# Where the attention's softmax rows are divided by their sums: on VectorE before the transposition, instead of on x^T after it

## The chip, the core and the metric

The kernel runs on one core of a Trainium2 chip. A core has five engines with a queue of instructions each: TensorE (PE, with its weight loads shown as PEld), VectorE (DVE), ScalarE (ACT), GpSimd (POOL) and SyncE (SP), which here issues nearly all DMAs. The engines run side by side and wait for each other only through semaphores. The metric is the device time of one execution in microseconds (us); lower is better.

## The reference

Three stages follow each other: causal attention with a decay for 2 batches of 8 heads, then a mixture of eight experts with weights from eight rounds of normalization, then a second mixture that sends each token to two experts. The change touches the first stage only:

```
scores = scale * q @ k^T + (cum[:, None] - cum[None, :])     # 576 x 576 for a head, future masked
attn = exp(scores - rowmax)
attn = attn / (attn.sum(-1) + 1e-09)
x = attn @ v                                                  # 576 x 64 for a head
```

The result of the sixteen heads, as rows of 512, is the input x of the first mixture.

## The kernel before

A head's 576 rows are five tiles (four of 128 rows and one of 64). Tile t keeps the columns up to its own diagonal, so it is 128, 256, 384, 512 or 576 wide, and it lies in the buffer P of its head (two buffers, for even and odd heads). For each tile PE multiplies q by k (`score_mm`, L253, in two parts for precision), VectorE adds the decay and takes the row minimum of the negated scores (`score_max`, L281, named CUSTOM_DVE in the trace and ISA in the program order), and ScalarE takes the exponential and sums it along the row (`score_exp`, L286). PE then transposes the tiles (`turn_mm`, L343) into PSUM tiles t, of which there are two: the first transposition of a head takes tiles 0 and 1 together, the next three take tiles 2, 3 and 4. ScalarE rounds what was transposed (`turn_hi`, L355), VectorE takes the remainder (`turn_lo`, L359), and only then is t free. PE multiplies by the parts of v (`value_mm`, L372), and VectorE collects x^T of two heads, a pair, in xf (`value_add`, L383).

The x^T of a pair is not yet divided. The sums of a head's rows lie along partitions, but x^T needs their reciprocals along the free axis. So `recip` (L323, L324) makes the reciprocals in a tile rs (two buffers), SP sends them to DRAM as single numbers of 4 bytes (L325, L326), `bcast` reads them back spread over 64 partitions (L332), and `x_mul` (L388) multiplies, on GpSimd for seven pairs and on VectorE for the last. Then `x_parts` (L397, L398) splits x^T into two rounded parts. GpSimd also splits q (`split_q`, L248, L249) and v (`split_v`, L235, L236).

The order on every engine is written out by hand: `at(time, fn)` puts each step at a place in fifths of a head, five to a head, and the steps are issued sorted by place. Engines work their queues strictly in that order. From head 10 on, PE also works on the first expert's first 384 tokens (`fill_mm`, L131 to L133, with names o<-xh,w1h), between the steps of the heads. When the last pair's x^T is split, PE goes on with the logits of the first gate (L567, L568) and the experts, which take the rest of the time.

Of the kernel before, what the change touches and what calls it, by code (L numbers as in the profile page):

```python
# [10 lines left out]
F32 = mybir.dt.float32  # L11
# [4 lines left out]
OP = mybir.AluOpType  # L16
# [4 lines left out]
# places of the attention's instructions, in fifths of a head's time  # L21
# [8 lines left out]
D_RECIP = 1.9  # L30
D_VAL = [[3.6, 4.8, 5.81, 5.82], [5.8, 6.2, 7.3, 7.66]]
D_X = [5.35, 9.05, 9.65]
D_SPLITV = 3.95
D_CONV = 1.25
# and of the first gate's, in us
T_GATE = [0.4, 1.85, 3.3, 3.55, 3.8, 1.8]
# and of the routing's after a tile's, in us
T_ROUTE = [[1.45, 1.8, 3.0, 5.75, 11.65, 0.4, 4.2], [2.0, 3.7, 4.0, 5.9, 6.85, 2.15, 5.55], [1.05, 1.6, 2.65, 6.2, 7.4, 0.4, 3.9], [1.0, 1.15, 2.3, 5.4, 7.15, 3.5, 0.6]]
# of the weights' conversions there, and of the first list's transposes
# [7 lines left out]
def attn_moe_moe2_kernel(ctx: ExitStack, tc: tile.TileContext, q, k, v, f, wg1, w1, w2,  # L47
                         wg2, wn2, noise, w21, w22, out, dbg=None):
    nc = tc.nc
# [5 lines left out]
    # slots of the second mixture's lists: of the first expert's tokens, early and late, and the others' in  # L55
    # the order of their length
# [25 lines left out]
    rscr = nc.dram_tensor("r_scratch", (B * H, S), F32, kind="Internal").ap()  # L82
# [52 lines left out]
    # what the gates need  # L135
# [19 lines left out]
    # ---------------------------------------------------------------- attention  # L155
    def attention():
        with ExitStack() as c2:
# [7 lines left out]
            # buffers with parts that stay zero  # L165
# [8 lines left out]
            def load_head(p, nm, hs, tail=True, views=(0, 1)):  # L174
                """rows of some heads of a pair; those past the fourth tile come for both"""
                b, pr = divmod(p, NP)
                src = {"q": q, "k": k, "v": v}[nm][b, 2 * pr:2 * pr + 2]
                if (p, nm) not in RAW:
                    RAW[p, nm] = (RV if nm == "v" else
                                  ap.tile([128, 5, 2, 2, 64], F32, name="raw_k", bufs=2) if nm == "k" else  # L180
                                  ap.tile([128, 5, 2, 64], F32, name="raw_q", bufs=2))
                r = RAW[p, nm]
                views = [r[:, :, :, z, :] for z in views] if nm == "k" else [r]
                for h in hs:
                    for x in views:
                        nc.sync.dma_start(x[:, 0:4, h, :], src[h, 0:512].rearrange("(c p) d -> p c d", p=128))
                if tail:
                    for x in views:
                        nc.sync.dma_start(x[0:64, 4, :, :], src[:, 512:576].rearrange("h p d -> p h d"))
# [11 lines left out]
            def spread_cum(c0, w):  # L201
                """the same for the first head, without the way over DRAM"""
                CP[c0] = ps.tile([128, 512], F32, name="t", bufs=2), w
                nc.tensor.matmul(CP[c0][0][:, :w], ident[0:NH, 0:1].to_broadcast([NH, 128]), cum[:, c0:c0 + w],
                                 start=True, stop=True)
# [5 lines left out]
            # minus the cumulated log decay of all heads, to be read back along the free axis  # L211
# [39 lines left out]
            XF, RB = {}, {}  # L251
# [36 lines left out]
            def prep_mm(n, nm):  # L288
                """transposed operands of a head in their parts, [q_hi; q_lo], [k_hi; k_hi], [k_lo; k_lo]"""
                p, h = divmod(n, 2)  # L290
                r = QS.pop(n) if nm == "q" else RAW[p, "k"][:, :, h].rearrange("p c z d -> p c (z d)")
                tag = {(0, "k"): "o", (1, "q"): "t", (1, "k"): "o"}.get((n, nm))
                if tag:
                    pts = [(ps.tile([128, 512], F32, name=tag, bufs=2), c0, w) for c0, w in ((0, 256), (256, 320))]
                else:
                    pts = [(ps.tile([128, 2, 512], F32, name="w", bufs=1).rearrange("p z x -> p (z x)"), 0, S)]
                for c in range(5):
                    m = 128 if c < 4 else 64
                    pt, c0, w = pts[(c > 1) * (len(pts) - 1)]
                    to, unit = pt[:, c * 128 - c0:c * 128 - c0 + m], ident[0:m, 0:m]  # L300
                    if nm == "q":
                        # rounded already
                        to, unit = to.bitcast(F32R), identr[0:m, 0:m]
                    nc.tensor.transpose(to, r[0:m, c, :], unit)
                PT[n, nm] = pts
# [14 lines left out]
            def recip(n):  # L320
                """1 / (sum + 1e-9) of a head's rows, sent out to be read back along the free axis"""
                rs = ap.tile([128, 5], F32, name="rs", bufs=2)
                nc.vector.tensor_scalar(rs, SUM[n % 2], 1e-9, None, op0=OP.add)  # L323
                nc.vector.reciprocal(rs, rs)  # L324
                nc.sync.dma_start(rscr[n, 0:512].rearrange("(t p) -> p t", p=128), rs[:, 0:4])  # L325
                nc.sync.dma_start(rscr[n, 512:576].rearrange("(t p) -> p t", p=64), rs[0:64, 4:5])  # L326

            def bcast(p):
                RB[p] = ap.tile([128, S], F32, name="rb", bufs=1)
                for h in range(2):  # L330
                    src = rscr[2 * p + h]
                    nc.sync.dma_start(RB[p][h * 64:h * 64 + 64, :],  # L332
                                      bass.AP(tensor=src.tensor, offset=src.offset, ap=[[0, 64], [1, S]]))

            def turn_mm(n, u):
                """transposes of a head's rows, the first two tiles together"""
# [24 lines left out]
            def value_mm(n, u, z):  # L361
                """a part of x^T of a head"""
# [22 lines left out]

            def x_mul(p):
                eng = nc.vector if p == NPT - 1 else nc.gpsimd
                eng.tensor_tensor(XF[p], XF[p], RB.pop(p), op=OP.mult)  # L388
# [27 lines left out]
            # the order of the work: five places to a head, fractions of them, over all heads  # L416
# [27 lines left out]
            for n in range(NH):  # L444
# [15 lines left out]
                at(g + D_RECIP, recip, n)  # L460
# [5 lines left out]
            for p in range(NPT):  # L466
                g = 10 * p
                at(g + 5 + D_X[0], bcast, p)
                at(g + 5 + D_X[1], x_mul, p)
                at(g + 5 + D_X[2], x_parts, p)  # L470
# [28 lines left out]
    # ---------------------------------------------------------------- experts  # L499
# [10 lines left out]
    def g1(ah, al, n, hh, hl, fcs=range(FC)):  # L510
        """hT = relu(w1^T x^T) in its two parts"""
# [17 lines left out]
    def g2(hh, hl, ts, mid=None):  # L529
        """y[tokens, DM] of the token columns ts of hT"""  # L530
# [7 lines left out]
    # ---- gate of the first mixture  # L538
# [4 lines left out]
    def first_units():  # L543
        """the gate, and beside its iterations the first expert's second unit and the first unit's way back"""
        with ExitStack() as c2:
# [79 lines left out]
            # times in us  # L625
# [23 lines left out]
    # ---------------------------------------------------------------- order of the experts' work  # L649
    # weights in the order of their use: the sixth expert's come twice, its last tokens after the seventh's  # L650
# [23 lines left out]
    # ---------------------------------------------------------------- second mixture: routing  # L674
    # lists of tokens: the first expert's early tokens, its late ones, then the others'
    # from the shortest to the longest; room for them in the table by expert
# [28 lines left out]
    # where the next token of each expert goes  # L705
# [4 lines left out]
    # counts above which a list has one more tile  # L710
# [11 lines left out]
    # on the way to or from a transposition  # L722
# [4 lines left out]
    # the two experts of the tokens of some tiles, with their weights, and their places in the lists  # L727
# [9 lines left out]
    def route_copy(t):  # L737
        """x^T of a tile, of the early ones in its two parts and in the place of the first mixture's"""
# [17 lines left out]
    def late_logits(t, t0):  # L756
        """the same on a shorter way, by more of the tensor engine's time"""
# [14 lines left out]
    def route_rank(t0, t1):  # L772
# [13 lines left out]
        # log1p(u) = log(w) - ((w - 1) - u) / w with w = 1 + u  # L786
# [11 lines left out]
        # how many experts come before each, by value and then by number  # L798
# [63 lines left out]
    def read_list(l):  # L862
        """the first entries of a list, as [slots of a tile, tiles, (token, weight)]"""
# [12 lines left out]
    def order_lists():  # L876
        """the experts from the second on by the number of their tokens"""
# [22 lines left out]
    def pick(l):  # L900
        """the expert of a list"""
# [3 lines left out]
    # ---------------------------------------------------------------- second mixture: experts  # L905
# [27 lines left out]
    def m2_g1(l, ht, fcs=range(FC)):  # L933
# [3 lines left out]
        # few tokens: they stay in the array, and the weights stream  # L937
# [17 lines left out]
    def m2_g2(l, ht, mid=None):  # L955
        """the way back of a list; y^T first where more work follows, so that all of the list's tokens stream"""
# [31 lines left out]
    def m2_out(l, t, py):  # L988
        """the tokens of a tile of a list, weighed, to the output"""
# [15 lines left out]
    # ---------------------------------------------------------------- the work in its order  # L1005
    def conv_next(s, which):
        """the weights of a stage in their parts, and the loads that follow them"""
# [6 lines left out]
    def last_units(i0):  # L1014
        """the rest of the first mixture, with the routing of its tokens as they are done"""
# [161 lines left out]
    # ---------------------------------------------------------------- tokens beyond the lists' first parts  # L1177
# [82 lines left out]
```

## Time and profile before

| | us |
|---|---|
| median of three runs | 1278.12 |
| lowest, highest run | 1276.38, 1281.51 |
| span of the profiled execution | 1280.1 |
| PE busy in the span | 1207.2 |
| VectorE busy in the span | 532.0 |
| first transposition of head 0 starts | 18.35 |
| first transposition of head 15 starts | 183.91 |
| last gate logits done, experts follow | 209.37 |

The execution's own time is given by its span, from its first to its last instruction; what lies around the span is not listed apart for it. The span lies between the lowest and the highest run. The attention is the first sixth of the execution, up to about 209 us. PE counts as busy while a matmul is under way, at whatever clock; the granted clock is a column of its own, 1.00 for 2.4 GHz and 0.50 for 1.2 GHz.

### The profile page before, as it was taken

To read this page: it belongs to the slowest core of one execution; us is meant where nothing else is said; L and a number is where in the kernel's file an instruction comes from. 1 tells how busy PE (TensorE), PEld (TensorE's weight loads), DVE (VectorE), ACT (ScalarE), POOL (GpSimd) and SP (SyncE) were. 2 spreads that over 40 slices of the span, in tenths; PEclk is the share of its full clock that TensorE was granted. 3 is DMA by queue.
4 is the path that set the end of the run, shared out by engine and by line. 5 is a ranking of instruction groups with operands and counts; after the bars stand their busy time and mean duration, and the time that the engine had idled before them with its cause. 6 is when DMAs were issued, how large, how long until landed. Compare 5 with 4: busy or idle time off the path is not lost. (4 is left out here: it accounts for less than half of the span.)

```text
span 1280.1 us, 17679 instructions
## 1 busy us (share of the span) xinstructions
PE 1207.2 (94%) x6965; PEld 1093.4 (85%) x6965; DVE 532.0 (42%) x1092; ACT 403.5 (32%) x796; POOL 184.0 (14%) x283
## 2 busy tenths in 40 slices
PE   8696779999999999999999999999999987999996
PEld 5575668999999999999999999899888867999995
DVE  6584554633133232232332332333354734565541
ACT  6684562112122121121221221222132432544440
POOL 4233422000000000000000000000012125343332
PEclk9897897999999999999999999999999998999999
DMA  7879964111020120220220220222020467576632
GB/s 127 126 109 91 87 59 136 50 66 51 16 66 23 45 66 1 66 67 1 66 67 1 66 66 1 66 67 66 26 72 29 165 173 205 178 222 216 198 105 61
DMA packets 123482, 107.73 MB, mean 84 GB/s; under 512 B 63086, under 2 KB 98030, under 8 KB 123391
## 3 DMA queue, kind: packets, MB, share of 16 engines
q1 hardware_dynamic: 110239, 92.26, 30.5%
q0 software_dynamic: 13152, 14.27, 4.1%
q8 instruction: 56, 0.92, 0.3%
q14 instruction: 35, 0.29, 0.1%
HBM read 96.83 MB, written 10.02 MB: 83 GB/s over the span
## 5 line engine op out<-in xcount | busy, mean ns | idle before, releaser
L131 PE MATMUL h<-xh,w1h 128*128 128x384 f32 (+8 forms) x1056 | 337.6, 320 | 1.1 <-DVE htl L520 1.0
L132 PE MATMUL h<-xl,w1h 128*128 128x384 f32 (+8 forms) x1056 | 335.1, 317 | 0.0
L133 PE MATMUL h<-xh,w1l 128*128 128x384 f32 (+8 forms) x1056 | 335.0, 317 | 0.0
L519 ACT ACTIVATE hth<-h 128x384 fp32r<-128x384 f32 (+8 forms) x264 | 119.2, 454 | 477.2 <-PE h L133 469.7
L525 PE MATMUL y<-w2h,hth 128*128 128x512 f32 (+1 forms) x624 | 245.1, 393 | 0.0
L526 PE MATMUL y<-w2l,hth 128*128 128x512 f32 (+1 forms) x624 | 244.1, 391 | 0.0
L527 PE MATMUL y<-w2h,htl 128*128 128x512 f32 (+1 forms) x624 | 244.0, 391 | 0.0
L520 DVE SCALAR_TENSOR_TENSOR htl<-h,hth 128x384 fp32r<-128x384 f32 (+8 forms) x264 | 132.8, 508 | 185.6 <-ACT hth L519 185.2
L131 PEld LDWEIGHTS h<-xh,w1h 128*128 128x128 f32 x1056 | 200.0, 189 | 3.4 <-DVE htl L520 1.8
L132 PEld LDWEIGHTS h<-xl,w1h 128*128 128x128 f32 x1056 | 200.0, 189 | 1.0
L133 PEld LDWEIGHTS h<-xh,w1l 128*128 128x128 f32 x1056 | 199.9, 189 | 0.0
L527 PEld LDWEIGHTS y<-w2h,htl 128*128 128x128 f32 (+1 forms) x624 | 117.2, 188 | 25.3 <-DVE htl L953 0.2
L525 PEld LDWEIGHTS y<-w2h,hth 128*128 128x128 f32 (+1 forms) x624 | 117.5, 188 | 23.8
L526 PEld LDWEIGHTS y<-w2l,hth 128*128 128x128 f32 (+1 forms) x624 | 117.4, 188 | 23.8
L853 POOL DMA_INDIRECT table_scratch<-rows,place x18 | 17.6, 977 | 785.5 <-DVE place L845 722.6
L671 DVE SCALAR_TENSOR_TENSOR acc<-y,Pgate,acc 128x512 f32<-128x512 f32 x52 | 39.0, 750 | 201.7 <-PE y L527 201.7
L127 DVE TENSOR_TENSOR w1l<-raw,w1h 128x1024 fp32r<-128x1024 f32 x68 | 83.4, 1227 | 75.9 <-ACT w1h L126 73.8
L126 ACT CAST w2h<-raw 128x1024 fp32r<-128x1024 f32 x68 | 70.1, 1053 | 94.9 <-PE y L527 91.0
L127 DVE TENSOR_TENSOR w2l<-raw,w2h 128x1024 fp32r<-128x1024 f32 x68 | 81.0, 1221 | 39.6 <-ACT w2h L126 37.6
L126 ACT CAST w1h<-raw 128x1024 fp32r<-128x1024 f32 x68 | 71.4, 1050 | 82.4 <-PE h L132 55.6
L343 PE MATMUL t<-ident,P 128*128 128x128 f32 (+1 forms) x240 | 37.5, 280 | 38.1 <-DVE ptla L359 36.7
L343 PEld LDWEIGHTS t<-ident,P 128*128 128x128 f32 (+1 forms) x240 | 25.7, 151 | 42.9 <-DVE ptla L359 38.1
(243 smaller groups left out, 1285.7 us busy)
## 6 DMA issues: line engine op xcount, KB each, us to landing
raw<-in_moe_w_dram SPq DMA_DIRECT2D x136, 512.0 KB
cb<-ncum_scratch SPq DMA_DIRECT2D x7, 576.0 KB
raw_k<-in_k_dram SPq DMA_DIRECT2D x30, 128.0 KB
rb<-r_scratch SPq DMA_DIRECT2D x16, 144.0 KB
out_dram<-zer SPq DMA_DIRECT2D x1, 2304.0 KB
x_scratch<-acc SPq DMA_DIRECT2D x9, 256.0 KB
raw_q<-in_q_dram SPq DMA_DIRECT2D x16, 128.0 KB
raw_v<-in_v_dram SPq DMA_DIRECT2D x16, 128.0 KB
```

The costliest lines, as they stand in the source:

```text
L126: nc.scalar.copy(hv, rv)
L127: nc.vector.tensor_tensor(lv, rv, hv.bitcast(F32), op=OP.subtract)
L131: nc.tensor.matmul(pt[:, :n], w1h[:, kc, fs], ah[:, kc, :], start=kc == 0, stop=False)
L132: nc.tensor.matmul(pt[:, :n], w1h[:, kc, fs], al[:, kc, :], start=False, stop=False)
L133: nc.tensor.matmul(pt[:, :n], w1l[:, kc, fs], ah[:, kc, :], start=False, stop=kc == KC - 1)
L343: nc.tensor.transpose(pt[:, c:c + m], P[0:m, POFF[t] + j * 128:POFF[t] + j * 128 + 128], ident[0:m, 0:m])
L519: nc.scalar.activation(hh[:, fc, :n], pt[:, :n], AF.Relu)
L520: nc.vector.scalar_tensor_tensor(hl[:, fc, :n], pt[:, :n], 0.0, hh[:, fc, :n].bitcast(F32), op0=OP.max, op1=OP.subtract)
L525: nc.tensor.matmul(py[:m], hh[:, fc, ts], w2h[:, fc, :], start=fc == 0, stop=False)
L526: nc.tensor.matmul(py[:m], hh[:, fc, ts], w2l[:, fc, :], start=False, stop=False)
L527: nc.tensor.matmul(py[:m], hl[:, fc, ts], w2h[:, fc, :], start=False, stop=fc == FC - 1)
L671: nc.vector.scalar_tensor_tensor(acc[:, t, :], py, P[:, t, e:e + 1], acc[:, t, :], op0=OP.mult, op1=OP.add)
```

## The change

`recip` is now done in two parts, for tiles 0 to 2 and for tiles 3 and 4. A new step `weigh` multiplies a tile of P in place by its rows' reciprocals on VectorE, one instruction for each of the five tiles, ahead of that tile's transposition. The way over DRAM (`rscr`, `bcast`) and `x_mul` are gone, and `x_parts` stands at place 13 of its pair instead of 14.65.

```
-D_RECIP = 1.9
+D_RECIP = [-0.35, 1.9]
+D_WEIGH = [-0.2, 0.0, 0.2, 2.0, 2.25]
-D_X = [5.35, 9.05, 9.65]
+D_X = 8.0
...
-            def recip(n):
-                rs = ap.tile([128, 5], F32, name="rs", bufs=2)
-                nc.vector.tensor_scalar(rs, SUM[n % 2], 1e-9, None, op0=OP.add)
+            def recip(n, t0, t1):
+                if t0 == 0:
+                    RS[n] = ap.tile([128, 5], F32, name="rs", bufs=2)
+                rs = RS[n][:, t0:t1]
+                nc.vector.tensor_scalar(rs, SUM[n % 2][:, t0:t1], 1e-9, None, op0=OP.add)
                 nc.vector.reciprocal(rs, rs)
-                nc.sync.dma_start(rscr[n, 0:512].rearrange("(t p) -> p t", p=128), rs[:, 0:4])
-                nc.sync.dma_start(rscr[n, 512:576].rearrange("(t p) -> p t", p=64), rs[0:64, 4:5])
...
-            def bcast(p):
-                RB[p] = ap.tile([128, S], F32, name="rb", bufs=1)
...
+            def weigh(n, t):
+                m = 128 if t < 4 else 64
+                x = PP[n % 2][0:m, POFF[t]:POFF[t] + (128 * (t + 1) if t < 4 else S)]
+                nc.vector.tensor_scalar(x, x, RS[n][0:m, t:t + 1], None, op0=OP.mult)
...
-            def x_mul(p):
-                eng = nc.vector if p == NPT - 1 else nc.gpsimd
-                eng.tensor_tensor(XF[p], XF[p], RB.pop(p), op=OP.mult)
...
-                at(g + D_RECIP, recip, n)
+                at(g + D_RECIP[0], recip, n, 0, 3)
+                at(g + D_RECIP[1], recip, n, 3, 5)
+                for t in range(5):
+                    at(g + D_WEIGH[t], weigh, n, t)
...
-                at(g + 5 + D_X[0], bcast, p)
-                at(g + 5 + D_X[1], x_mul, p)
-                at(g + 5 + D_X[2], x_parts, p)
+                at(g + 5 + D_X, x_parts, p)
```

The order of PE's and ScalarE's instructions stays as it was. On VectorE, before, between the splitting of head 1's fourth tile and head 2's first transposed tiles (P_104 and sums_107 belong to even heads, P_105 to odd ones):

```order
L359 TENSOR_TENSOR ptlb<-t,pthb 128x4x128
L281 ISA P_104,nm<-w,cb 64x576
L281 ISA nm 64x1
L359 TENSOR_TENSOR ptlb<-t,pthb 128x5x64
L383 TENSOR_TENSOR xf<-o,tmp 64x256
L281 ISA P_105,nm<-s,cb 128x128
L281 ISA nm 128x1
L281 ISA P_105,nm<-s,cb 128x256
L281 ISA nm 128x1
L323 TENSOR_SCALAR rs<-sums_107 128x5
L324 RECIPROCAL rs<-rs 128x5
L359 TENSOR_TENSOR ptla<-t,ptha 128x384
```

The first half of the same stretch now (the lines below L320 stand some lines higher in the changed file):

```order
L358 TENSOR_TENSOR ptlb<-t,pthb 128x4x128
L325 TENSOR_SCALAR rs<-sums_107 128x3
L326 RECIPROCAL rs<-rs 128x3
L332 TENSOR_SCALAR P_104<-P_104,rs 128x128
L332 TENSOR_SCALAR P_104<-P_104,rs 128x256
L332 TENSOR_SCALAR P_104<-P_104,rs 128x384
L281 ISA P_104,nm<-w,cb 64x576
```

Five instructions have come in ahead of the fifth tile's `score_max`. The second half, up to the same transposed tiles:

```order
L281 ISA P_105,nm<-s,cb 128x256
L281 ISA nm 128x1
L325 TENSOR_SCALAR rs<-sums_107 128x2
L326 RECIPROCAL rs<-rs 128x2
L332 TENSOR_SCALAR P_104<-P_104,rs 128x512
L332 TENSOR_SCALAR P_104<-P_104,rs 64x576
L358 TENSOR_TENSOR ptla<-t,ptha 128x384
```

Two wide multiplications have come in between the reciprocals and the splitting that frees the PSUM tile t. On SP's queue, before, around the reciprocals of heads 0 and 1:

```order
L189 DMA raw_v<-in_v_dram 64x2x64
L325 DMA r_scratch<-rs 128x4x1
L326 DMA r_scratch<-rs 64x1
L198 DMA cb<-ncum_scratch 128x1152
L325 DMA r_scratch<-rs 128x4x1
L326 DMA r_scratch<-rs 64x1
L186 DMA raw_q<-in_q_dram 128x4x64 x2
```

And now:

```order
L189 DMA raw_v<-in_v_dram 64x2x64
L198 DMA cb<-ncum_scratch 128x1152
L186 DMA raw_q<-in_q_dram 128x4x64 x2
L189 DMA raw_q<-in_q_dram 64x2x64
L186 DMA raw_k<-in_k_dram 128x4x64 x4
```

Of SP's 48 DMAs for the reciprocals (16 times L325 and L326, and 16 times L332) none is left, and the loads of a pair follow each other directly.

## Rows read from the trace of the kernel before

**Rows 1.** The page: granted clock of PE in 40 slices of the span.
```profile
PEclk9897897999999999999999999999999998999999
```

**Rows 2.** Waits of the engines, 18 to 210 us (total, times, longest).
```profile
DVE rs L323 <- DMA r_scratch<-rs: 52.4, 10, 11.3
...
POOL qs L248 <- DMA raw_q<-in_q_dram: 36.7, 4, 14.7
PE t L343 <- DVE ptla L359: 36.7, 9, 9.8
```

**Rows 3.** Waits of SP's own queue, 18 to 210 us.
```profile
SPq L186 <- DMA r_scratch<-rs: 33.7, 7, 6.8
```

**Rows 4.** Windows of 4 us around head 0's reciprocals: busy times, PEclk, DMA share, GB/s.
```profile
20.00:24.00 4.00, 3.86 (x28) 2.74 (x27) 3.38 (x9) 3.75 (x12) 1.62 (x4) 1.00 0.89 173
24.00:28.00 4.00, 4.00 (x33) 3.64 (x34) 3.05 (x13) 3.35 (x9) 1.65 (x2) 1.00 1.48 44
```

**Rows 5.** Windows of one head without stall: PE, PEld, DVE, ACT, POOL busy.
```profile
33.08:40.62 7.54, 7.54 (x58) 6.22 (x58) 6.59 (x21) 6.86 (x20) 0.00 (x0) 1.00 0.98 101
...
164.27:173.90 9.63, 9.63 (x70) 8.27 (x70) 6.75 (x20) 7.36 (x20) 4.53 (x5) 1.00 0.48 46
```

**Rows 6.** Timeline of PE: start, us, instruction, idle time before it and its releaser.
```profile
18.35 0.50 PE L343 MATMUL t<-ident,P 128*128 128x128 f32 x3
...
62.28 1.11 PE L343 MATMUL t<-ident,P 128*128 128x128 f32 x4 [9.79 <-DVE ptla L359]
...
125.88 0.85 PE L343 MATMUL t<-ident,P 128*128 128x128 f32 x3
...
173.90 0.50 PE L343 MATMUL t<-ident,P 128*128 128x128 f32 x3
...
183.91 0.49 PE L343 MATMUL t<-ident,P 128*128 128x128 f32 x3
...
190.75 0.66 PE L343 MATMUL t<-ident,P 128*128 128x128 f32 x4 [4.21 <-DVE ptla L359]
...
206.75 0.34 PE L567 MATMUL h<-xh,wgs 128*16 128x384 f32 x1 [2.10 <-ACT xh L394]
```

**Rows 7.** Windows after idle times of PE, the tail, and what follows it.
```profile
120.00:124.00 4.00, 4.00 (x20) 3.07 (x19) 3.25 (x9) 2.47 (x7) 0.13 (x1) 0.50 0.58 146
...
176.00:180.00 4.00, 1.73 (x12) 1.27 (x10) 1.64 (x5) 1.46 (x6) 0.00 (x0) 1.00 0.55 80
183.91:209.37 25.46, 18.69 (x96) 15.43 (x95) 8.26 (x18) 5.85 (x13) 6.19 (x42) 0.85 0.25 59
...
209.37:215.30 5.93, 5.93 (x25) 5.26 (x25) 1.67 (x6) 0.44 (x1) 2.20 (x47) 0.50 0.53 194
```

**Rows 8.** VectorE's groups by shape, 18 to 200 us (count, busy us, mean ns).
```profile
L281 DVE CUSTOM_DVE_ANT_0 P<-s,cb 128x512 f32<-128x512 f32 x15 | 10.2, 681 | 0.0
...
L127 DVE TENSOR_TENSOR w1l<-raw,w1h 128x1024 fp32r<-128x1024 f32 x4 | 5.1, 1270 | 0.0
...
L281 DVE CUSTOM_DVE_ANT_0 P<-s,cb 128x128 f32<-128x128 f32 x15 | 4.2, 282 | 0.2
...
L324 DVE RECIPROCAL rs<-rs 128x5 f32<-128x5 f32 x16 | 3.1, 191 | 0.6
```

**Rows 9.** Timeline of VectorE: two conversions from SBUF to SBUF.
```profile
6.14 0.21 DVE L67 CAST identr<-ident 128x128 fp32r<-128x128 f32 x1
6.28 0.21 DVE L69 CAST identb<-ident 128x128 bf16<-128x128 f32 x1
```

**Rows 10.** Timelines of VectorE and GpSimd: L323 alone, and beside a GpSimd instruction.
```profile
33.73 0.17 DVE L323 TENSOR_SCALAR rs<-sums 128x5 f32<-128x5 f32 x1
...
70.43 2.41 POOL L236 TENSOR_TENSOR vs<-raw_v,vs 128x640 fp32r<-128x640 f32 x1
...
71.35 1.52 DVE L323 TENSOR_SCALAR rs<-sums 128x5 f32<-128x5 f32 x1
```

**Rows 11.** Window of one pair's run of work on GpSimd, `split_v` to `split_q`.
```profile
95.90:103.70 7.80, 2.12 (x16) 1.65 (x15) 0.00 (x0) 2.95 (x8) 7.23 (x9) 0.95 0.56 52
```

More of the change, by code (lines that the diff above doesn't have):

```diff
@@ L81, in attn_moe_moe2_kernel @@
     nc.scalar.preload_act_table_set("natural_log_exp_and_others")
-    rscr = nc.dram_tensor("r_scratch", (B * H, S), F32, kind="Internal").ap()
     E2 = 2 * E
@@ L249, in split_q @@
                         nc.gpsimd.tensor_tensor(lo, src, hi.bitcast(F32), op=OP.subtract)
-            XF, RB = {}, {}
+            XF, RS = {}, {}
             def score_mm(n, t):
@@ L318, in prep_lo @@
                 OPS[n]["l"] = lo
-            def recip(n):
-                rs = ap.tile([128, 5], F32, name="rs", bufs=2)
-                nc.vector.tensor_scalar(rs, SUM[n % 2], 1e-9, None, op0=OP.add)
-                nc.vector.reciprocal(rs, rs)
-                nc.sync.dma_start(rscr[n, 0:512].rearrange("(t p) -> p t", p=128), rs[:, 0:4])
-                nc.sync.dma_start(rscr[n, 512:576].rearrange("(t p) -> p t", p=64), rs[0:64, 4:5])
-            def bcast(p):
-                RB[p] = ap.tile([128, S], F32, name="rb", bufs=1)
[L330 to L333, printed above, removed]
+            def recip(n, t0, t1):
[3 more added lines that the diff above has]
+                nc.vector.tensor_scalar(rs, SUM[n % 2][:, t0:t1], 1e-9, None, op0=OP.add)
+                nc.vector.reciprocal(rs, rs)
+            def weigh(n, t):
+                m = 128 if t < 4 else 64
+                x = PP[n % 2][0:m, POFF[t]:POFF[t] + (128 * (t + 1) if t < 4 else S)]
+                nc.vector.tensor_scalar(x, x, RS[n][0:m, t:t + 1], None, op0=OP.mult)
             def turn_mm(n, u):
```

## The prediction

> **What bounds the kernel now.** I read the page's PEclk line first [rows 1]: PE's granted clock is below full in slices of the first sixth and near the end, so PE is interrupted there, and the first sixth is what the change touches. Next the waits of that stretch [rows 2]. VectorE stood 52.4 us in ten waits at L323, the first instruction of `recip`, until a DMA of rs to DRAM had landed: rs has two buffers, and the sums of head n may not overwrite the reciprocals of head n-2 before SP has sent them. Behind L323 on VectorE stands the splitting of `ptla`, which frees the PSUM tile t, and PE stood 36.7 us in nine waits for it. One look at PE's timeline shows such a wait: 9.79 us ahead of the third transposition of head 4 [rows 6]. Third, SP's own queue [rows 3]: seven times a load of k or q stood until one of the 4-byte DMAs had landed, 33.7 us. The windows show why they are slow [rows 4]: ahead of the first of them the DMA engines move 173 GB/s at a share of 0.89, and with it under way 44 GB/s at a share of 1.48. So the chain is: slow sends of reciprocals, late loads and late sends behind them in SP's queue, rs not free, VectorE, PE. Heads without such a wait take 7.54 us, with PE busy in all of it, ScalarE in 6.86 and VectorE in 6.59; with the first expert's matmuls between, 9.63 us, VectorE 6.75 [rows 5].
>
> **What goes.** All 48 DMAs of the reciprocals, and with them the wait at L323: rs is then read and written on VectorE alone. Without anything put in their place the heads would come every 7.54 and 9.63 us. The load of a pair was fast before the first send [rows 4], so I take no new wait for loads; the rival for that is below. `x_mul` goes from GpSimd, and at the end from VectorE, where the last pair's waited for its read from DRAM: PE stood 2.10 us there [rows 6].
>
> **What comes.** VectorE gets seven instructions more in a head: a second sum and reciprocal, 0.17 + 0.19 = 0.36 us [rows 8, 10], and five `weigh`. The trace has no wide TENSOR_SCALAR from SBUF to SBUF, so both ends are from the nearest rows. At one column for each step, as `score_max` shows, 128 columns take 0.282 us and each further one 1.04 ns ((681 - 282) / 384) [rows 8], so 0.28 + 0.42 + 0.55 + 0.68 + 0.75 = 2.67. At two columns a step, as the conversion of 128 columns in 0.21 us suggests [rows 9], with half the slope, 0.21 + 0.28 + 0.34 + 0.41 + 0.44 = 1.68. Neighbours overlap by 0.07 (0.21 long, 0.14 apart [rows 9]), so 0.35 goes off each. I take the second, since a multiplication by one number a row is nearer to a conversion, with one stream, than to `score_max`, with two: 1.33 + 0.36 = 1.7 us a head; the other end is 2.7.
>
> The Trainium skill (VectorE: DVE Perf Modes, section "The perf-mode tier table") says the same of fp32 `tensor_scalar` between SBUF operands: twice the rate. No run here shows it yet.
>
> With that VectorE needs 6.59 + 1.7 = 8.3 us for a head where PE needs 7.54: it becomes the engine that sets the pace of heads 0 to 9. In heads 10 to 14 it needs 6.75 + 1.7 = 8.45 and lies under PE's 9.63. The conversions of the first expert's weights (L127, 1.27 us each [rows 8]) fall on heads 5, 7, 9 and 11; where VectorE sets the pace they count in full.
>
> **A port shared with GpSimd.** L323 takes 0.17 us alone, but 1.52 us when it was issued at 71.35 while GpSimd was in `split_v`; it ended with that instruction (70.43 + 2.41 = 72.84) [rows 10]. So this narrow instruction, from SBUF to SBUF, stood until GpSimd was done. `weigh` is of the same kind, so seven instructions a head can meet this. GpSimd works in runs: nine instructions in 7.23 us, 0.80 each [rows 11], of which one (`x_mul`) goes. In the changed order such a run is let off by `value_add` of an odd head, which VectorE does early in the even head after it; the next odd head's two groups of `weigh` come into its later part and into the `split_q` behind it, while an even head's groups find GpSimd idle. Bounds for a pair: 0, if none meets; 7 x 0.80 = 5.6, if each stands a whole instruction. I take half, 2.8 for a pair, 1.4 for a head, as one comes on average in the middle of the other; for heads 0 to 3, where `split_q` and `split_v` alone are there, 0.7.
>
> This is also where the Trainium skill speaks against the change (SBUF — State Buffer, section "Who interferes with whom"): a two-column instruction of VectorE and any of GpSimd exclude each other for the whole instruction. The row of 1.52 us agrees. By that page an instruction at one column a step with one SBUF input would not be held.
>
> **The sum**, by the starts of first transpositions [rows 6]. Head 0 at 18.35 as before. Heads 0 to 3: 4 x (8.3 + 0.7) = 36.0. Heads 4 to 9: 6 x (8.3 + 1.4) + 3 x 1.27 = 62.0. Head 10 then starts at 116.4, against 125.88: 9.5 less. Heads 10 to 13: 4 x (8.45 + 1.4) + 1.27 = 40.7, to 157.1, against 173.90. Head 14 has no k to split (576 columns, 0.75): 9.1, so head 15 starts at 166.2 against 183.91, 17.7 less. In the tail the 4.21 and 2.10 us of idle go [rows 6], since nothing of DRAM is waited for and x^T of the last pair is split under the remaining matmuls of the first expert. After the idle times PE ran at 0.50: the tail's mean of 0.85 over 25.46 us is 3.8 us of lost clock [rows 7], of which I take 3, and of the 5.93 us behind it, all at 0.50, 2 of the 3 lost. That is 11.3 more, 29.0 in all. What follows is bound by PE [rows 1] and moves up as it is. The profiled span is 1280.1, 2.0 above the median of the three runs and inside them; off the median, 1278.1 - 29.0 = 1249.
>
> **Rivals.**
> (a) The two engines hardly meet on the port. Then 10 x 8.3 + 3.8 = 86.8 to head 10, 4 x 9.63 = 38.5 and 8.9 to head 15, at 152.6: 31.3 + 11.3 less, 1235.5. For it: GpSimd is idle in about half of a pair's time. Against it: VectorE is busy nearly always, so a run of 7 us finds a `weigh`.
> (b) Every meeting costs a whole GpSimd instruction, 2.8 us a head: 4 x 9.7 + (6 x 11.1 + 3.8) + (4 x 11.25 + 1.3) + 10.5 brings head 15 to 184.4, so only the tail's 11.3 is left, 1267. For it: in the row of 1.52 us the waiting GpSimd instruction came before the waiting VectorE one, so they may alternate.
> (c) `weigh` at one column a step and no meeting: 9.3 a head, 96.8 to head 10, 38.5 and 8.9: 1245.5, the forecast's time by another way.
> (d) Slower: the late loads are not the sends' doing. GpSimd stood 36.7 us for q [rows 2], and if a pair's twelve loads alone need longer than two heads take, PE's waits stay under another name, and VectorE's extra work comes on top: 10 x (0.8 + 1.1) for heads 0 to 9 and some 1 for the others, less the 2.10 at the end, +18, 1296. It decides once a pair's loads land more than about 15 us after their issue. Against it: 173 GB/s ahead of the first send [rows 4].
> (e) Slower by the clock: PE now idles 1 to 2 us in each head. The 2.27 us of idle in 176 to 180 us left the clock at 1.00, while 120 to 124 us, behind one of the nine long waits, ran at 0.50 [rows 7]; with 0.50 in each head the time would be beyond 1300.
>
> **How the numbers follow.** Forecast, with between a quarter and three quarters of the meetings (1238 to 1258): 0.58; (c), with the same time, 0.04; (a) 0.16; (b) 0.14; (d) 0.05; (e) 0.01; and 0.02 for no clear change, between (b) and (d). From 1232 to 1264 I leave out (d), (e), the upper end of (b) and little below (a), some 2 in 10. A difference of 0.5%, 6.4 us, is about what a measurement can tell from none here: faster than 1271.7 has 0.92, within it 0.02, slower 0.06.
>
> **What would show it.** Right: no wait for r_scratch, no PE wait above some 3 us between 18 us and the gate, PEclk at 1.00 through the attention, heads 0 to 9 at 8 to 10 us with VectorE busy nearly throughout, `weigh` of 512 columns at 0.41 us where GpSimd is idle and longer by up to 1.6 us where it isn't, in odd heads above all. Wrong: PE waiting for q, k or cb (then (d)); `weigh` at 0.68 us and never longer (then (c)); heads of 11 us with GpSimd and VectorE in turn (then (b)).

## The result, and the profile after

The changed kernel takes 1255.79 us (median of four, 1254.44 to 1257.79), the kernel before 1277.25 beside it (1275.81 to 1281.51): a ratio of 0.9823, 95% interval 0.9802 to 0.9844. That is 21.5 us faster; the forecast was 1249, with 29 us less, and a range of 1232 to 1264. The profiled execution of the changed kernel has a span of 1256.1 us against 1280.1, so the two traces differ by 24.0.

Lines of the changed kernel are shifted: `weigh` is L332, the two `recip` instructions L325 and L326, `turn_mm` L342, `turn_lo` L358, `x_parts` L392 and L393. The page's slices of VectorE and of PE's granted clock, which answer to [rows 1]:

```profile
DVE  6999876423323323223233132333455653655541
...
PEclk9988899999999999999999999999999998999998
```

VectorE is now busy nine tenths or more in three of the slices with the heads; the clock is still below nine tenths in three, against the forecast of 1.00 throughout. The waits of the engines from 18 to 210 us (total, times, longest), for [rows 2]:

```profile
ACT P L286 <- DVE nm L281: 26.9, 21, 3.7
...
PE w L304 <- DVE nm L281: 9.7, 10, 1.9
PEld w L304 <- POOL vs L236: 8.6, 4, 2.1
```

No wait for r_scratch or q is left, and for k one of 0.3 us. ScalarE and PE now wait for `score_max` on VectorE: that of the row tile 4 stands behind the first three `weigh`, and its end frees the PSUM tile w. The third row names GpSimd, but its waits end with PE's for `score_max`: one at 88.57, where L236 had ended at 87.57. SP's own queue, for [rows 3]:

```profile
SPq L198 <- DVE nm L281: 32.2, 4, 9.8
SPq L106 <- DVE rs L325: 24.5, 2, 13.7
```

SP waits for buffers that VectorE, and in places PE, gives free and for no DMA; for what it loads only GpSimd waits longer than 0.3 us, once, 2.6 us for v. The window in which the DMA engines moved 44 GB/s at a share of 1.48 [rows 4] is now nearly free of transfers:

```profile
24.00:28.00 4.00, 4.00 (x31) 3.13 (x29) 3.87 (x9) 2.99 (x10) 2.29 (x2) 1.00 0.12 27
```

Two heads in the middle, an even and an odd one (PE, PEld, DVE, ACT, POOL busy, PEclk, DMA share, GB/s), and the tail, for [rows 5, 7]:

```profile
77.00:86.00 9.00, 8.01 (x59) 6.21 (x57) 8.74 (x25) 7.82 (x19) 4.39 (x8) 1.00 0.36 80
86.00:97.70 11.70, 9.53 (x57) 7.53 (x58) 11.56 (x30) 6.98 (x18) 4.63 (x5) 0.85 0.52 141
...
172.60:188.03 15.43, 15.29 (x97) 12.66 (x96) 8.70 (x19) 6.00 (x13) 3.98 (x79) 1.00 0.25 92
```

VectorE is busy in 8.74 of 9.00 and 11.56 of 11.70 us: it sets the pace. Where an odd head's time goes is seen in its timeline on VectorE, with the first three `weigh` of a head (x3), the other two (x2) and the reciprocals' first instruction:

```profile
17.66 1.35 DVE L332 TENSOR_SCALAR P<-P,rs 128x128 f32<-128x128 f32 x3
...
26.35 2.00 DVE L332 TENSOR_SCALAR P<-P,rs 128x128 f32<-128x128 f32 x3
...
44.79 2.91 DVE L332 TENSOR_SCALAR P<-P,rs 128x128 f32<-128x128 f32 x3
...
79.33 0.91 DVE L332 TENSOR_SCALAR P<-P,rs 128x512 f32<-128x512 f32 x2
...
84.08 0.55 DVE L325 TENSOR_SCALAR rs<-sums 128x3 f32<-128x3 f32 x1
...
84.88 2.91 DVE L332 TENSOR_SCALAR P<-P,rs 128x128 f32<-128x128 f32 x3
...
89.67 1.21 DVE L127 TENSOR_TENSOR w1l<-raw,w1h 128x1024 fp32r<-128x1024 f32 x1
...
91.40 1.25 DVE L332 TENSOR_SCALAR P<-P,rs 128x512 f32<-128x512 f32 x2
...
96.25 0.15 DVE L325 TENSOR_SCALAR rs<-sums 128x3 f32<-128x3 f32 x1
...
96.65 0.88 DVE L332 TENSOR_SCALAR P<-P,rs 128x128 f32<-128x128 f32 x3
...
104.80 0.55 DVE L325 TENSOR_SCALAR rs<-sums 128x3 f32<-128x3 f32 x1
...
126.90 2.92 DVE L332 TENSOR_SCALAR P<-P,rs 128x128 f32<-128x128 f32 x3
```

and on GpSimd in the same time:

```profile
83.39 0.40 POOL L248 CAST qs<-raw_q 128x256 fp32r<-128x256 f32 x1
...
85.12 0.71 POOL L235 CAST vs<-raw_v 128x640 fp32r<-128x640 f32 x1
85.92 1.65 POOL L236 TENSOR_TENSOR vs<-raw_v,vs 128x640 fp32r<-128x640 f32 x1
89.60 1.54 POOL L248 CAST qs<-raw_q 128x256 fp32r<-128x256 f32 x1 [2.03 <-PE w L304]
91.22 0.72 POOL L249 TENSOR_TENSOR qs<-raw_q,qs 128x256 fp32r<-128x256 f32 x1
```

The same three instructions take 0.88 us at 96.65, with GpSimd idle, and 2.91 at 84.88: the last of them ends some 0.2 us after L236 of GpSimd does (85.92 + 1.65 = 87.57, 84.88 + 2.91 = 87.79). L236 touches nothing that `weigh` reads or writes, so an engine can hold up another without a semaphore between them. By the starts of heads' first transpositions, the stages stand side by side like this (us):

| stage | before | forecast | after |
|---|---|---|---|
| heads 0 to 3 | 30.9 | 36.0 | 38.1 |
| heads 4 to 9 | 76.6 | 62.0 | 63.2 |
| heads 10 to 14 | 58.0 | 49.8 | 53.2 |
| head 15 to the end of the gate's matmuls | 25.5 | 16.2 | 15.4 |
| from there to the end | 1070.7 | 1068.7 | 1068.1 |

### The profile page after: what moved, and what is told of

Same layout as the page of the kernel before. It is cut to its first block, busy times and chain, and to the rows that moved or that the text cites. A ratio compares the mean times of both kernels' runs of the same rounds, so it can differ in the third digit from the quotient of the medians.

```text
span 1256.1 us, 17681 instructions
## 1 busy us (share of the span) xinstructions
PE 1206.5 (96%) x6965; PEld 1089.3 (87%) x6965; DVE 575.2 (46%) x1203; ACT 402.8 (32%) x796; POOL 178.0 (14%) x276
## 5 line engine op out<-in xcount | busy, mean ns | idle before, releaser
L127 DVE TENSOR_TENSOR w1l<-raw,w1h 128x1024 fp32r<-128x1024 f32 x68 | 83.1, 1223 | 75.7 <-ACT w1h L126 73.2
L127 DVE TENSOR_TENSOR w2l<-raw,w2h 128x1024 fp32r<-128x1024 f32 x68 | 81.0, 1221 | 39.9 <-ACT w2h L126 37.9
L969 PE MATMUL y<-htl,w2h 128*128 128x282 f32 (+5 forms) x192 | 58.3, 303 | 0.7 <-DVE htl L516 0.7
L967 PE MATMUL y<-hth,w2h 128*128 128x282 f32 (+5 forms) x192 | 58.7, 306 | 0.0
```

Of the source, the lines that this page charges most:

```text
L127: nc.vector.tensor_tensor(lv, rv, hv.bitcast(F32), op=OP.subtract)
L967: nc.tensor.matmul(py[:, :caps[l]], w2h[:, fc, dsl], ht[0][:, fc, :caps[l]], start=fc == 0, stop=False)
L969: nc.tensor.matmul(py[:, :caps[l]], w2h[:, fc, dsl], ht[1][:, fc, :caps[l]], start=False, stop=fc == FC - 1)
```

## The experiments

The kernel before took 1287 to 1290 us in the comparisons that follow, on three chips, so each result is given as a ratio to the runs of it on the same chip. The changed kernel there (e5): 0.977.

**What the division costs.** The five `weigh` are left out, all else of the changed kernel stays; the rows stay undivided.

```
-                for t in range(5):
-                    at(g + D_WEIGH[t], weigh, n, t)
```

> The changed kernel without its five multiplications a head (the rows stay undivided, the reciprocals are made and not used). Theory P: VectorE's work in the heads, and the port it shares with GpSimd, is all that keeps the heads from 7.54 and 9.63 us, and loads land in time once nothing is sent to DRAM. Then heads 0 to 9 take 7.5 to 8.0 us, heads 10 to 13 9.6 to 10.0, head 15 starts near 144 us instead of 172.6, and the time is about 1227 us (1222 to 1234). Rival L: the loads of q, k and cb are late by themselves, and VectorE hides that now; then PE or GpSimd waits for loads, and the time stays above 1240 us.

1227.61 us, ratio 0.9518 (0.946 to 0.9577). The windows of one head without and one with the first expert's matmuls:

```profile
40.50:48.00 7.50, 7.50 (x58) 6.17 (x57) 7.23 (x22) 7.04 (x19) 3.12 (x5) 1.00 0.78 197
105.30:114.90 9.60, 9.60 (x70) 8.24 (x70) 8.21 (x23) 8.20 (x21) 2.21 (x4) 1.00 0.66 159
```

PE has no gap in either, at 7.5 and 9.6 us as [rows 5]. So what PE lost before was lost by the way over DRAM, the loads alone are fast enough (197 GB/s here), and the division costs 2.5% (0.977 to 0.952), half of what the removal gains.

**Is it rs with its two buffers?** The kernel before, with sixteen.

```
-                rs = ap.tile([128, 5], F32, name="rs", bufs=2)
+                rs = ap.tile([128, 5], F32, name="rs", bufs=16)
```

> The kernel before with sixteen buffers for the reciprocals instead of two, nothing else. Theory S: the slow sends cost time only through the two buffers; then VectorE never waits for a send, heads 0 to 9 come every 7.54 us, the tail still waits for the last pair's way over DRAM, and the time is about 1235 us, less than the changed kernel's 1255.8. Rival L2: the sends also hold up the loads behind them in SP's queue; then the wait moves to q, k or cb, and the time is 1255 to 1272 us.

1288.89 us, ratio 0.9997 (0.9974 to 1.0019): nothing. VectorE's wait at L323 is gone and the same time stands elsewhere, from 18 to 210 us:

```profile
POOL qs L248 <- DMA raw_q<-in_q_dram: 57.8, 5, 15.3
POOL xf L388 <- DMA rb<-r_scratch: 24.5, 2, 17.2
...
DVE P L281 <- DMA cb<-ncum_scratch: 18.9, 3, 8.3
```

The longest wait of the profile before was not the cause but the first place at which late sends were noticed.

**Is it the sends or what reads them back?** e1 with the sends put back, sixteen buffers, and nobody who reads them.

```
-                    RS[n] = ap.tile([128, 5], F32, name="rs", bufs=2)
+                    RS[n] = ap.tile([128, 5], F32, name="rs", bufs=16)
...
+                if t1 == 5:
+                    nc.sync.dma_start(rscr[n, 0:512].rearrange("(t p) -> p t", p=128), RS[n][:, 0:4])
+                    nc.sync.dma_start(rscr[n, 512:576].rearrange("(t p) -> p t", p=64), RS[n][0:64, 4:5])
```

> No weigh, so the rows stay undivided (left out); but the reciprocals go out to DRAM again by the 32 small DMAs of the kernel before (rs with 16 buffers), and nobody reads them back. Without the sends this was 1227.6 us. Theory 'the sends': 576 packets of 4 bytes a head slow every load behind them, as the windows at 44 GB/s and a share of 1.48 show; pairs' loads then land late again, PE waits of 5 to 15 us for q, k or cb, and the time is 1260 to 1285. Rival 'the read-back': what held up SP's queue was the read of r_scratch that waits for the sends (38.5 us of SP's queue with 16 buffers of rs); with no read-back the loads are behind nothing that waits, and the time is 1228 to 1240.

1268.88 us, ratio 0.9861 (0.9809 to 0.9914): 3.4% more than e1 by the ratios, for 32 DMAs whose data nobody wants. SP's queue, and the window behind the first send:

```profile
SPq L187 <- DMA r_scratch<-rs: 36.5, 8, 7.1
```

```profile
24.00:28.00 4.00, 4.00 (x32) 3.76 (x32) 3.93 (x14) 3.45 (x9) 2.85 (x4) 1.00 1.60 36
```

The loads at L187 need nothing that a send writes, and yet eight of them start only when one has landed. As in [rows 4] the DMA engines are occupied by 4-byte packets and move little. Whether it is the engines' own queues or SP's that is full, or a wait in the program, the trace does not tell, so that stays open. The sends alone bring back 3.4 of the 4.8% between e1 and the kernel before; the rest goes with what e6 leaves out, the read-back and `x_mul`.

**The same sums in larger packets.** The kernel before, x^T by reciprocals, but each head's are turned on PE into five rows and sent as one DMA of five runs of 512 bytes; rs has four buffers, which by e2 is worth nothing.

```
+            def row_mm(n):
+                ...
+                nc.tensor.transpose(pt[0:5, 640:768], RS[n][1], ident)
+            def row_out(n):
+                ...
+                nc.vector.tensor_copy(row, pt[0:5, 640:768])
+                nc.sync.dma_start(rscr[n].rearrange("(t p) -> t p", p=128), row)
```

> The kernel before, x^T by reciprocals through DRAM, but each head's reciprocals are turned on PE into five rows (128x5 to 5x128, into 128 unused columns of a PSUM tile), copied once by VectorE and sent by one DMA of 5 rows of 512 bytes in place of 576 packets of 4 bytes. Theory 'the sends': the small packets alone made the loads late; heads then come every 7.6 us and 9.7 us (VectorE about 6.9, no division of rows), 1230 to 1238, faster than both kernels. Rival 'the way over DRAM': a read-back in SP's queue that waits for the send, or the last pair's product that waits for it, holds up loads and tail whatever the packets' size; 1250 or more.

1235.66 us (1231.62 to 1238.77), ratio 0.960 (0.9553 to 0.9646): faster than both kernels, with the round trip kept. The same window moves 154 GB/s at a share of 0.57:

```profile
24.00:28.00 4.00, 4.00 (x32) 3.70 (x32) 3.96 (x12) 3.26 (x8) 2.77 (x4) 1.00 0.57 154
```

So it is the small packets that made the kernel before slow: with larger ones the read-back stays and costs little (e10, below, is 0.3% behind e1). Their number and their size changed together, and two DMAs a head became one, so these three are not told apart. The Trainium skill (DMA: Bandwidth & Descriptors, "Rules for kernel authors") says that a last dimension with a stride becomes one descriptor for each element and advises to arrange it contiguously. The profiles agree: 63086 packets under 512 bytes in the kernel before and 53438 here are 603 fewer for each of the 16 heads, whose 576 numbers had gone out one by one.

Heads 0 to 9 took 8.0 to 8.6 us there, not the 7.6 expected, and the new copy stood 9.3 us in ten waits on VectorE:

```profile
DVE row L337 <- ACT k L310: 9.3, 10, 1.4
```

So one more, with the copy placed behind the splitting of k's low part.

```
-                at(g + 3.07, row_out, n)
+                at(g + 3.8, row_out, n)
```

> The kernel with the reciprocals turned into rows (ratio 0.960), its copy `row_out` two instructions later on VectorE, behind the splitting of k's low part, since the copy stood 9.3 us in ten waits for a copy of k by ScalarE and what is behind it on VectorE with it. Theory 'VectorE's wait': heads 0 to 9 go from 8.2 to some 7.7 us, up to 5 us faster, ratio 0.956. Rival 'another engine is as late': ScalarE's and GpSimd's work or PE's PSUM tiles hold the same pace; within 2 us, ratio 0.958 to 0.962.

1229.72 us (1229.07 to 1232.74), ratio 0.9543 (0.9509 to 0.9578). Heads 0 to 9 come every 7.7 us, those with L127 8.4. It is the fastest complete kernel of this study, 2.3% below the changed one by the ratios, and 0.3% behind e1, which divides nothing.

**Does GpSimd hold `weigh`?** The changed kernel, with a row sum that nobody reads added to each `weigh`.

```
-                nc.vector.tensor_scalar(x, x, RS[n][0:m, t:t + 1], None, op0=OP.mult)
+                un = ap.tile([128, 1], F32, name="un", bufs=4)
+                nc.vector.tensor_scalar(x, x, RS[n][0:m, t:t + 1], None, op0=OP.mult, op1=OP.add, accum_out=un[0:m])
```

> The changed kernel with a row sum taken along in each of the five multiplications (its result is not used), which by the Trainium skill (SBUF - State Buffer, section Who interferes with whom) keeps the instruction from using the shared port. Theory P (odd heads lose about 3.6 us of a pair on the port): the multiplications go at one column a step, some 1.0 us more a head, but none is held by GpSimd: even and odd heads alike near 9.5 us, a pair 19.1 instead of 20.7, the time about 1248 us (1243 to 1253). Rival W (the odd heads lose by where the multiplications stand, ahead of the instruction that frees the PSUM tile w, and not by the port): 1.0 us more in each of 15 heads, about 1267 us.

1257.09 us, ratio 0.9757 (0.9708 to 0.9806), the changed kernel's 0.977 within what can be told. But the time is made up otherwise. The same three tiles of an odd head on VectorE, with GpSimd in L235 and L236 from 84.81 to 87.15 beside them:

```profile
83.75 0.55 DVE L325 TENSOR_SCALAR rs<-sums 128x3 f32<-128x3 f32 x1
...
84.56 0.35 DVE L333 TENSOR_SCALAR_CACHE_REDUCE P<-P,rs 128x128 f32<-128x128 f32 x1
...
84.83 0.48 DVE L333 TENSOR_SCALAR_CACHE_REDUCE P<-P,rs 128x256 f32<-128x256 f32 x1
...
85.22 0.61 DVE L333 TENSOR_SCALAR_CACHE_REDUCE P<-P,rs 128x384 f32<-128x384 f32 x1
```

They take 1.29 us with the reading of the last sum (84.56 to 85.85) where the plain form took 2.91, and no longer in an odd head than in an even one; L325, left as it was, is still held, 0.55 against 0.15 alone. Undisturbed, the plain form is the faster: the same three take 0.88. So the plain form is fast and held, this one slow and free, and over a pair they are worth the same. This is what the Trainium skill says (SBUF — State Buffer, "Who interferes with whom") of `tensor_scalar` with and without the accumulator's output; both rows agree.

**Another engine.** The first three `weigh` of a head on ScalarE.

```
-                nc.vector.tensor_scalar(x, x, RS[n][0:m, t:t + 1], None, op0=OP.mult)
+                if t < 3:
+                    nc.scalar.activation(x, x, AF.Copy, scale=RS[n][0:m, t:t + 1])
+                else:
+                    nc.vector.tensor_scalar(x, x, RS[n][0:m, t:t + 1], None, op0=OP.mult)
```

> The changed kernel with the first three tiles multiplied on ScalarE instead of VectorE, at the same places. Theory P: VectorE is left with about 7.75 us a head, the odd heads lose on the port only for the last two tiles (about 1.2 us a pair), ScalarE goes from 6.86 to about 8.4 us: a pair takes 17 to 17.7 us instead of 20.7, the time is about 1238 us (1233 to 1244). Rival C: ScalarE's queue is tied to VectorE's so closely that 1.5 us more on it delay the exponentials and the splitting as much as they save; then 1250 to 1260 us.

1261.82 us, ratio 0.9795 (0.9741 to 0.9848). Heads 0 to 9 take 9.5 to 11.0 us, odd or even. VectorE is held less (its L325 with three columns and the tile of 512 columns still are in places, 337 and 595 ns in the mean, where alone they take 150 and 485), and ScalarE's own queue comes in the place of it.

```profile
PEld o L374 <- ACT pthb L357: 23.7, 16, 2.1
ACT P L333 <- DVE rs L326: 18.7, 15, 1.9
...
PE o L374 <- ACT pthb L357: 16.3, 10, 2.0
```

`pthb`, which PE needs next, stands behind the three, and they behind the reciprocal.

**The place.** The changed kernel once more (e5), and with its first three `weigh` behind `score_max` of tile 4 (e7).

```
-D_WEIGH = [-0.2, 0.0, 0.2, 2.0, 2.25]
+D_WEIGH = [0.53, 0.54, 0.55, 2.0, 2.25]
```

> The changed kernel once more, on the chip that times the three kernels beside it, so that it can be compared with them and, by the ratio to the kernel before, with the earlier runs. Expected: the ratio of the first measurement, 0.982 (0.980 to 0.984); 0.975 to 0.977 would say that dividing at one column a step (ratio 0.9757) gained nothing over it.

> The first three weigh of a head go from -0.2, 0.0 and 0.2 to 0.53, 0.54 and 0.55 of the order's units, behind the score_max of tile 4 that frees PSUM tile w for PE (9.7 us of waits of PE on it in the changed kernel, and 26.9 of ScalarE on score_max). Theory 'VectorE and the port': VectorE is busy 3.9 of 4 us, so another order takes nothing off its sum; within 4 us of the changed kernel. Rival 'place': PE's late weights and the clock that falls behind them are the cost of the order; 6 to 10 us faster than the changed kernel.

1256.52 us, 0.977 (0.9724 to 0.9816), and 1245.97 us (1245.55 to 1246.73), 0.9685 (0.9645 to 0.9725): 10.5 us for three numbers. I had expected no gain, since VectorE is busy anyway; that was wrong, because the time of `weigh` is not a constant. The groups of `weigh` from 18 to 190 us in the changed kernel (count, busy us, mean ns), and then in e7:

```profile
L332 DVE TENSOR_SCALAR P<-P,rs 128x384 f32<-128x384 f32 x16 | 13.0, 814 | 0.0
L332 DVE TENSOR_SCALAR P<-P,rs 128x512 f32<-128x512 f32 x16 | 10.1, 633 | 0.6
L332 DVE TENSOR_SCALAR P<-P,rs 128x128 f32<-128x128 f32 x15 | 9.2, 616 | 0.5
L332 DVE TENSOR_SCALAR P<-P,rs 64x576 f32<-64x576 f32 x16 | 8.1, 504 | 0.0
L332 DVE TENSOR_SCALAR P<-P,rs 128x256 f32<-128x256 f32 x16 | 6.0, 374 | 0.0
```

```profile
L332 DVE TENSOR_SCALAR P<-P,rs 128x384 f32<-128x384 f32 x16 | 11.7, 729 | 0.0
L332 DVE TENSOR_SCALAR P<-P,rs 128x512 f32<-128x512 f32 x16 | 9.1, 566 | 0.6
L332 DVE TENSOR_SCALAR P<-P,rs 64x576 f32<-64x576 f32 x16 | 8.2, 514 | 0.0
L332 DVE TENSOR_SCALAR P<-P,rs 128x128 f32<-128x128 f32 x16 | 5.5, 345 | 0.0
L332 DVE TENSOR_SCALAR P<-P,rs 128x256 f32<-128x256 f32 x16 | 5.4, 340 | 0.0
```

Over the five shapes they were busy 46.4 us (46.9 in e5, with all sixteen of the first shape) and are busy 39.9: in their new place they meet less of GpSimd's run of work. That is about 7 of the 10.5 us; ScalarE's wait of 26.9 us for `score_max` and PE's 9.7 for the tile w shrink as well, to 4.9 and nothing listed. To tell the port from the freed PSUM tile w, both edits together:

> Both edits at once: dividing at one column a step (with a row sum that nobody reads, ratio 0.9757 alone) and the first three weigh behind the score_max of tile 4 (0.9685 alone; the changed kernel 0.977 on that chip). Theory 'the place matters by the port': moved back, group A meets less of GpSimd's run of work (2.40 us in place of 2.91 in an odd head, group B 0.91 in place of 1.25); at one column a step there is no meeting, so the move is worth nothing more: ratio 0.974 to 0.978, some 1256. Rival 'the place matters by PSUM tile w': PE and ScalarE get the maximum of tile 4 earlier whatever the division costs, and the move is worth its 10 us here too: ratio 0.966 to 0.969, some 1246.

1254.51 us, ratio 0.9744 (0.9701 to 0.9786), the ratio of one column a step alone. ScalarE's wait for `score_max` falls here too, from 24.8 us in e3 to 2.8, and PE's for tile w from 7.1 to nothing listed, and the time is the same. Where `weigh` meets nobody its place is worth nothing, so in e7 it was worth its 10 us by the port and what follows from it, and not by those waits.

## Why the prediction was right, and where it was off

**What goes: right, with one wrong link.** No wait for r_scratch or q is left, and the loads are not late by themselves (e1), so rival (d) falls. The chain began rightly with slow sends, but put rs and VectorE between them and PE as if the chain needed both. e2 shows that it doesn't: with rs free at all times the sends hold up the loads, and the time is the same. "Without anything put in their place the heads would come every 7.54 and 9.63 us" is what e1 measured, 7.5 and 9.6.

**What comes: right in kind, each size somewhat low.** Two columns a step was the right choice, and e3 is its other end. The three and the two `weigh`, undisturbed, take 0.88 and 0.91 us (at 96.65 and 79.33), where I had 0.69 and 0.78 by the same overlaps. VectorE's loop without disturbance is 8.55 us (96.25 to 104.80, from one L325 to the next) in place of 8.3.

**The port: the price near, the heads not.** Heads 4 and 5, and 6 and 7, take 20.7 us a pair: 2 x 8.55 for the loop, 1.21 for L127 in the odd head, and 2.4 are left for the port, 2.8 forecast. The forecast's pair was 20.7 as well, but by luck: its loop was 0.5 too short for two heads and its port 0.4 too dear, and 2.8 was only the middle of 0 and 5.6. Odd heads bear most of it, as forecast (11.70 us, of which 1.21 are L127, and 9.00). That stage came out at 63.2 against 62.0; 1.0 of the difference is head 9, below. For heads 0 to 3 I took half the price, since only `split_q` and `split_v` run there. But these are the ones that meet `weigh`: the three take 1.35, 2.00 and 2.91 us for heads 0, 1 and 3 (at 17.66, 26.35 and 44.79). Four loops of 8.55 are 34.2 of the 38.1 us, which leaves 3.9 for the port and the start of head 0, about 1.0 a head.

**The step that failed: heads 10 to 13 under PE's 9.63 us.** I let VectorE's 8.45 + 1.4 = 9.85 stand as a head's time. It comes in uneven pieces: 2.92 us for one group at 126.90 put `fill_lo` (htl) off, PE stood 2.21 us for it, and the granted clock fell behind that. PE's timeline there, and two windows:

```profile
130.43 1.56 PE L371 MATMUL o<-pthb,vs 128*128 128x320 f32 x5 [2.21 <-DVE htl L404]
```

```profile
128.00:132.00 4.00, 1.79 (x9) 1.69 (x8) 3.89 (x9) 2.19 (x4) 1.60 (x1) 0.70 0.02 7
132.00:136.00 4.00, 4.00 (x19) 3.72 (x19) 3.34 (x8) 1.55 (x3) 1.86 (x4) 0.50 0.96 224
```

Heads 10 and 11 took 24.5 us together against the 21.0 of the sum, and that is the stage's 3.4, as heads 12 to 14 nearly even out. The same wait is there in e5, 2.32 us long, with 23.8 us for the two heads. So rival (e) was there in a small part, where PE had matmuls enough to lose by a slow clock. Between heads 4 and 9 the clock fell too: at 0.85 in heads 5 and 7 it cost nothing that VectorE did not cost already, but head 9, at 0.73, took 12.75 us in place of 11.71, and VectorE waited 0.45 us for PE there. In e5 head 9 ran at 0.85 and took 11.71, so this part differs from one execution to the next. e7, with less of the port, has a mean clock of 1.00 in 118 to 172 us (0.94 in the changed kernel).

**The tail: right.** 15.4 us against 16.2 and then 1068.1 against 1068.7; the clock is 1.00 from 172.6 on, so the 4.21, 2.10 and the lost clock all went. The sum of the misses is 2.1 + 1.2 + 3.4 - 0.8 - 0.6 - 0.2 (head 0 starts that much earlier) = 5.1, which but for rounding is the 29.0 less the 24.0 of the traces. The medians differ by 2.5 less than the spans, since the profiled execution of the kernel before lay further above its median than that of the changed one. How near the 29 us came is known no better than the kernel before is: beside e5 the change gained 30.4 us (1286.87 to 1256.52).

**The rivals.** (a), no meeting, 1235.5, was too good by the port's price; (b), a whole instruction each, 1267, too bad. (c) forecast the time by another way, and was wrong as a mechanism: `weigh` is held. e3, which is that mechanism, took the changed kernel's time, with heads of 9.6 us where no L127 stands, against 9.3 in that sum.

## What to carry to other kernels

Before a way over DRAM is replaced by arithmetic on the busiest vector engine, look at its packets: one transposition on PE and a DMA of contiguous runs took away the same stalls as the change did, at 0.28 us of VectorE a head for its copy in place of 2.9 for `weigh` (46.4 us by 16), and was 2.3% faster. The longest wait in a profile may only be where lateness is first met; giving its buffer more room tells, and costs one line. Where a fast form of instruction excludes another engine, its place against that engine's runs of work counts as well (in e7 10.5 us of the 29 that the division costs by e1 and e5), and "VectorE is busy anyway" is no reason that a move is worth nothing.

## What the runs showed of the hardware that was not expected

- Exclusion works both ways: a GpSimd conversion of 128x256, 0.40 us alone, took 1.54 at 89.60, beside VectorE's L127 from SBUF to SBUF, and ended 0.26 us after that (90.88). I had priced only what VectorE loses; GpSimd's lateness is not seen to keep another engine of the changed kernel waiting.
- The kernel before took 1277 us in one comparison and 1287 to 1290 in three others; the changed one 1256 beside the first and beside one of the others, so its ratio is 0.982 by the one and 0.977 by the other. The intervals, 0.9802 to 0.9844 and 0.9724 to 0.9816, overlap a little. Why the kernel before is slower in the later ones, and the changed one is not, no run here shows.
